# The start of a convolution-and-MLP kernel: first fifteen blocks in groups of five, x ahead of the third w_in chunk, more dummy matmuls, band cast on ScalarE

## The chip, the cores and the metric

One core of one Trainium2 chip. The metric is the device time of one execution in microseconds (us), lower is better. The kernel before took 723.87 us (median of three runs, 723.49 to 724.0).

## The reference, cut to what matters

```python
# a causal convolution of width 7 over the sequence, one softmaxed filter per head, 8 heads of 24 channels
w = softmax(weight)                                   # [8, 7]
y[b, s, h, :] = sum_k w[h, k] * x_pad[b, s + k, h, :] # x: [8, 4096, 192]
# an MLP without biases on its result
h = y.reshape(32768, 192) @ w_in                      # [192, 2048]
g = h * cos(h)
out = g @ w_out                                       # [2048, 192]
```

## The kernel before: the parts that the change touches

Two sequences of the batch are worked on side by side, one in each half of the 128 partitions ("lanes"). The convolution is a matmul with a banded matrix (`band`) over blocks of 112 positions; 37 blocks make a sequence. Eight 64-channel slices of blocks ("a pair") fill one PSUM bank per lane. A group of eight blocks gives three pairs; a group of five gives two, one of 28 matmuls (channel slices 0 and 1 of four blocks) and one of 40 (the fifth block and slice 2):

```python
def group(b, k, n):
    if n == 5:
        pairs.append([(b, k + j, c) for c in range(2) for j in range(4)])
        pairs.append([(b, k + 4, c) for c in range(NCH)] + [(b, k + j, 2) for j in range(4)])
    elif n == 2:
        ...
    else:
        pairs.extend([(b, k + j, c) for j in range(n)] for c in range(NCH))
    loads.extend((b, k + j, min(4, n - j)) for j in range(0, n, 4))   # x comes in loads of up to 4 blocks

for b in range(HB):
    k = 0
    for n in [8] * (NBLK // 8) + [5] if b else [5, 8, 2] + [8] * ((NBLK - 21) // 8) + [6]:
        group(b, k, n)
        k += n
```

The order of the loads on SyncE's queue (every buffer is one of eight staging buffers; w_in comes in four chunks, w_out in two):

```python
load_blocks(*loads[0], (nc.sync, nc.scalar)); load_blocks(*loads[1])
load_w1(0); load_w1(1)
load_w1(2)
load_ahead(1)          # the x of the next pair: both loads of the eight-group
...
load_w1(3); load_w2(0); load_w2(1)
```

The rest is a hand-made schedule. Each letter emits one step: `U` an up-projection (6 matmuls, one of 512 positions by 128 hidden columns on both lanes), `S` its cosine on ScalarE, `M` the product on VectorE, `C`/`c` the two halves of a pair's convolution, `e` its copy out of PSUM and its transposing DMA into `cT`, `p` the cast of another pair's x and the loads for the next, `d` one of the sixteen parts of a down-projection (8 matmuls), `x`/`y` the stores, `k` the next of the jobs of `later()`, which are all on GpSimd or SyncE:

```python
def later():
    yield from (lambda c=c, q=q: cast_w1(c, q) for c in range(1, 3) for q in range(NCH))
    yield cast_pair
    yield lambda: load_ahead(3)
    yield cast_pair
    yield cast_pair
    yield from (lambda q=q: cast_w1(3, q) for q in range(NCH))
    yield from (lambda c=c, q=q: cast_w2(c, q) for c in range(2) for q in range(4))

fill("kkkUSMUSMUSMkkkUSMUSMUSMkkUSMUSMCceUSMkkkkkCceUSMUSMkkkkkkkkCceUSMU")
for k in range(NSETS - 2):
    emit("dddSMdUdMSUdSdMUdSMd" + ("p" if k == 0 else "") + "UdMSUdSdMCcdedMUdpSdUyxUMS")
```

I call the part up to the first `d` the fill and each pass of the loop a turn (8 `U`, 16 `d`). The down-projection changes between two PSUM banks, and at each changeover TensorE waits for a "mark", a 1x1 memset on GpSimd; GpSimd does its casts and marks in program order. And SyncE issues x loads, transposes and stores from one queue, also in program order.

## Time and profile before

| what | value | where from |
|---|---|---|
| time | 723.87 us | median of 3 runs |
| TensorE busy | 708.5 of 722.6 us | busy table |
| TensorE first useful up-projection | 12.67 us | timeline |
| first down-projection | 32.50 us | timeline |
| turns 2, 3, 4 start | 43.46, 54.37, 65.27 us | timeline |

From the first down-projection on, a turn takes 10.9 us and TensorE has no gap in it. (The times of a trace are of one execution; that of the kernel before took 724.41 us.)

### The profile page before, as it was taken

Reading aid. Unit: us, or ns where it says so; the run is one execution under the profiler, and the core shown is the slowest. Engines: PE = TensorE matmul, PEld = TensorE weight load, DVE = VectorE, ACT = ScalarE, POOL = GpSimd, SP = SyncE. Lnnn points to the kernel's source line nnn. Section 1 sums busy time; section 2 is a strip of 40 time slices with the busy share of each in tenths; the row PEclk is TensorE's granted clock in tenths of the full one; section 3 lists DMA queues with packets and bytes.
Section 4 is the critical chain, followed back from the end, with each engine's and each line's share of the span. In section 5 each row is a group of like instructions: output and inputs, shape, how many; then the busy total and the mean of one; then the engine's idle time right before and its main releaser. Section 6 shows DMA issues by size and latency. Waiting matters only on the chain.

```text
span 722.6 us, 27515 instructions
## 1 busy us (share of the span) xinstructions
PE 708.5 (98%) x12284; PEld 527.0 (73%) x12284; DVE 641.3 (89%) x594; ACT 589.1 (82%) x641; POOL 95.0 (13%) x345
## 2 busy tenths in 40 slices
PE   7799999999999999999999999999999999999997
PEld 5477777777777777777777777777777777777776
DVE  5799899999989999898898998998998999999994
ACT  4788888888888888888888888888888888778773
POOL 4510111110110111111101111101101100000000
PEclk9999999999999999999999999999999999999999
DMA  9956333552827337254653554516273321011102
GB/s 233 239 124 149 83 90 101 113 128 67 159 37 158 53 106 158 63 129 99 116 129 83 93 111 108 137 58 159 49 146 82 85 64 56 27 43 45 46 25 67
DMA packets 126339, 72.58 MB, mean 100 GB/s; under 512 B 52428, under 2 KB 124684, under 8 KB 126220
## 3 DMA queue, kind: packets, MB, share of 16 engines
q1 hardware_dynamic: 125386, 70.23, 42.4%
q8 instruction: 96, 1.57, 0.9%
q10 hardware_dynamic: 834, 0.59, 0.3%
q14 instruction: 23, 0.19, 0.1%
HBM read 33.48 MB, written 25.17 MB: 81 GB/s over the span
## 4 chain that ended last, share of the span: by engine, by line
PE 96%; DMA 3%; SPq 1%; DVE 0%; ACT 0%; issue 0%; POOL 0%; POOLq 0%
PE h L286 49%; PE acc L286 46%; DMA xw<-in_x_dram 2%; DMA xw<-in_moe_w_in_dram 1%; SPq L110 0%; DVE g L396 0%; SPq L232 0%; ACT cos L391 0%; POOL xb L161 0%; SPq L230 0%; DVE osb L433 0%; ACT osb L433 0%; SPq L104 0%; POOLq L542 0%; POOL mark L296 0%
## 5 line engine op out<-in xcount | busy, mean ns | idle before, releaser
L396 DVE TENSOR_TENSOR g<-h,cos 128x1024 bf16<-128x1024 f32 x512 | 603.8, 1220 | 30.1 <-ACT cos L391 23.4
L391 ACT ACTIVATE cos<-h 128x1024 bf16<-128x1024 f32 x512 | 511.1, 1023 | 106.7 <-PE h L286 87.5
L286 PEld LDWEIGHTS <-g 64*128 64x128 bf16 x8192 | 353.1, 94 | 102.3 <-POOL mark L296 2.2
L286 PE MATMUL acc<-w,g 64*128 64x192 bf16 x8064 | 415.3, 243 | 0.3 <-POOL mark L296 0.3
L286 PE MATMUL h<-cT,w 64*128 64x512 bf16 x3072 | 409.3, 378 | 2.2 <-DVE g L396 2.1
L286 PEld LDWEIGHTS <-w 64*128 64x128 bf16 x3072 | 148.4, 94 | 79.6 <-issue 5.8
L296 POOL MEMSET mark<- 1x1 f32 x192 | 16.9, 88 | 602.6 <-PE acc L286 593.8
L433 DVE COPY osb<-acc 128x384 f32<-128x384 f32 x63 | 35.1, 558 | 39.6 <-PE acc L286 39.6
L161 POOL CAST xb<-xw 128x512 bf16<-128x512 f32 (+1 forms) x113 | 64.7, 603 | 13.1 <-DMA xw<-in_x_dram 11.9
L344 ACT CAST ct<-h 112x1024 bf16<-112x1024 f32 (+2 forms) x53 | 52.5, 990 | 8.8 <-PE h L286 5.0
L286 PEld LDWEIGHTS <-band 64*128 64x128 bf16 x952 | 31.3, 96 | 5.0 <-issue 4.1
L433 ACT COPY osb<-acc 128x384 f32<-128x384 f32 x63 | 29.8, 473 | 5.7 <-PE acc L286 5.7
L286 PE MATMUL h<-xb,band 64*128 64x192 bf16 (+10 forms) x912 | 34.2, 214 | 0.0
L235 POOL CAST w<-xw 128x512 bf16<-128x512 f32 x12 | 6.9, 613 | 5.3 <-DMA xw<-in_moe_w_in_dram 5.3
L286 PE MATMUL h<-w,g 64*128 64x192 bf16 x128 | 5.9, 243 | 0.3 <-POOL mark L296 0.3
L183 PE MATMUL acc<-unit 128*112 128x112 bf16 x46 | 4.8, 302 | 1.3 <-POOL unit L166 1.3
L286 PE MATMUL acc<-xb,band 64*128 64x192 bf16 (+2 forms) x40 | 2.5, 260 | 3.5 <-POOL xb L161 3.4
L342 ACT CAST ct<-acc 112x512 bf16<-112x512 f32 x6 | 3.2, 592 | 3.0 <-PE acc L286 3.0
L183 PEld LDWEIGHTS <-unit 128*112 128x112 bf16 x46 | 4.4, 211 | 1.4 <-POOL unit L166 1.3
L245 POOL CAST w<-xw 128x384 bf16<-128x384 f32 x8 | 3.7, 507 | 0.3 <-DMA xw<-in_moe_w_out_dram 0.3
L196 ACT ACT_TABLE_LOAD x1 | 1.3, 1283 | 2.6 <-issue 2.6
L344 DVE CAST ct<-h 112x896 bf16<-112x896 f32 x1 | 1.1, 1091 | 2.1 <-PE h L286 2.1
(37 smaller groups left out, 18.7 us busy)
## 6 DMA issues: line engine op xcount, KB each, us to landing
out_dram<-osb SPq DMA_DIRECT2D x63, 384.0 KB, 2.9
xw<-in_x_dram SPq DMA_DIRECT2D x62, 384.0 KB, 6.3
xw<-in_x_dram SPq DMA_DIRECT2D x7, 336.0 KB, 4.2
xw<-in_moe_w_in_dram SPq DMA_DIRECT2D x4, 512.0 KB, 7.7
xw<-in_moe_w_out_dram SPq DMA_DIRECT2D x2, 768.0 KB, 8.9
cT<-ct SPq DMA_TRANSPOSE x66, 2.7
xw<-in_moe_w_in_dram SPq DMA_DIRECT2D x8, 128.0 KB, 8.4
xw<-in_x_dram SPq DMA_DIRECT2D x2, 192.0 KB
```

The lines of the kernel that those rows point to most:

```text
L161: copies[j % len(copies)](out=xbs[p][:, s0:s1], in_=src)
L183: nc.tensor.matmul(out=acc[0][0:W, 0:W], lhsT=unit, rhs=unit, start=True, stop=True)
L196: nc.scalar.activation(out=wex, in_=wq, func=AF.Exp)
L235: copy(out=w1[:, q, c * CW:(c + 1) * CW], in_=staged[1, c][:, q, :])
L245: nc.gpsimd.tensor_copy(out=w2[:, c * n:(c + 1) * n, :][:, fs, :], in_=staged[2, c][:, fs, :])
L286: ins = nc.tensor.matmul(out=o, lhsT=w, rhs=r, start=start, stop=stop, skip_group_check=True)
L296: ins = nc.gpsimd.memset(mark, 0.0)
L342: copy(out=ct[0:W, 0:n, s, :], in_=bank[0:W, 0:n * L].rearrange("p (j c) -> p j c", c=L))
L344: copy(out=ct[0:W, 0:n].rearrange("p j s c -> p s j c"), in_=ps[0:W, :, 0:n * L].rearrange("p s (j c) -> p s j c", c=L))
L391: nc.scalar.activation(out=cos, in_=hs[n], func=AF.Sin, bias=math.pi / 2.0, scale=1.0)
L396: nc.vector.tensor_tensor(out=g, in0=hs.pop(n), in1=cs.pop(n), op=ALU.mult)
L433: copy(out=osbs[k][:, 2 * bank:2 * bank + 2, :].rearrange("p a d -> p (a d)"), in_=src[:, 0:2 * D])
```

## The change

Its intent: convolve less before the up-projections can go on (the first pair of a group of five needs four blocks' x, 786 KB, that of a group of eight needs eight), have that x on the way before the third chunk of w_in, keep the clock that TensorE is granted up with more dummy matmuls, whose results nobody reads, and free VectorE of one copy.

```diff
-        for n in ... [5, 8, 2] + [8] * ((NBLK - 21) // 8) + [6]:
+        for n in ... [5, 5, 5] + [8] * ((NBLK - 21) // 8) + [6]:
...
-    keep_warm(30)
+    keep_warm(56)
...
-    nc.vector.tensor_copy(out=band[:, :, V:W], in_=spread)
-    keep_warm(16)
+    nc.scalar.copy(out=band[:, :, V:W], in_=spread)
+    keep_warm(20)
...
+    load_ahead(1)
     load_w1(2)
-    load_ahead(1)
+    load_ahead(2)
...
     def later():
-        yield from (lambda c=c, q=q: cast_w1(c, q) for c in range(1, 3) for q in range(NCH))
+        yield from (lambda q=q: cast_w1(1, q) for q in range(NCH))
         yield cast_pair
-        yield lambda: load_ahead(3)
+        yield from (lambda q=q: cast_w1(2, q) for q in range(NCH))
         yield cast_pair
-        yield cast_pair
+        yield lambda: load_ahead(2)
...
-    fill("kkkUSMUSMUSMkkkUSMUSMUSMkkUSMUSMCceUSMkkkkkCceUSMUSMkkkkkkkkCceUSMU")
-    for k in range(NSETS - 2):
-        emit("dddSMdUdMSUdSdMUdSMd" + ("p" if k == 0 else "") + "UdMSUdSdMCcdedMUdpSdUyxUMS")
+    fill("kkkUSMUSMUSMkUSMUSMkkkUSCceMUSMUSMkUSMkUSCceMUSMkkkkkkkkkkkUSMU")
+    emit("dddSMdUdMpSUdSdMUdSMdUdMSCcpUedSdMCcdedMUdpSdUyxUMS")
+    for k in range(1, NSETS - 2):
+        emit("dddSMdUdMSUdSdMUdSMdUdMSUdSdMCcdedMUdpSdUyxUMS")
```

More of the change, by code (lines that the diff above doesn't have):

```diff
@@ L129 @@
         k = 0
-        for n in [8] * (NBLK // 8) + [5] if b else [5, 8, 2] + [8] * ((NBLK - 21) // 8) + [6]:
+        for n in [8] * (NBLK // 8) + [5] if b else [5, 5, 5] + [8] * ((NBLK - 21) // 8) + [6]:
             group(b, k, n)
```

## The prediction

> **What bounds the kernel now.** I read the page first: the busy table and the chain that ended last.
>
> ```profile
> PE 708.5 (98%) x12284; PEld 527.0 (73%) x12284; DVE 641.3 (89%) x594; ACT 589.1 (82%) x641; POOL 95.0 (13%) x345
> PE 96%; DMA 3%; SPq 1%; DVE 0%; ACT 0%; issue 0%; POOL 0%; POOLq 0%
> ```
>
> TensorE is busy 98% of the span and is 96% of the chain, so the steady state is a TensorE program. The diff touches only the start. A start-up change can return just the time in which TensorE does no useful work there, so the second view was a table of windows over the first 45 us (columns: window, length, busy us and count of PE, PEld, DVE, ACT, POOL, then granted clock, DMA share, GB/s).
>
> ```profile
> 12.70:24.50 11.80, 7.77 (x48) 3.06 (x48) 9.70 (x9) 8.05 (x8) 4.07 (x7) 1.00 1.09 247
> 24.50:25.44 0.94, 0.00 (x1) 0.00 (x1) 0.02 (x1) 0.00 (x0) 0.67 (x2) 1.00 1.09 341
> 26.10:29.50 3.40, 3.38 (x30) 1.73 (x28) 1.23 (x1) 3.14 (x5) 3.40 (x7) 0.50 1.10 346
> 34.47:45.00 10.53, 10.53 (x215) 8.25 (x212) 9.73 (x10) 9.07 (x10) 2.17 (x7) 1.00 0.77 166
> ```
>
> From 34.47 us on TensorE never stops. Before that there are three losses: 12.70 to 24.50 it is one third idle, at 24.50 to 25.44 every compute engine but GpSimd stands still, and from 26.10 to 29.50 it runs at half clock. What holds it is told by the chain of waits in order of time (start, length, what):
>
> ```profile
> 13.31 11.34 DMA xw<-in_x_dram
> ...
> 24.77 0.62 POOL xb L161
> 25.39 0.04 issue
> 25.44 0.62 PE acc L286 x12
> ...
> 29.52 1.03 ACT cos L391
> 30.56 0.02 issue
> 30.58 1.24 DVE g L396
> 31.82 0.04 issue
> 31.86 0.82 PE h L286 x6
> ```
>
> So the third group of pairs (an eight-block group, whose x fills two staging buffers and stands behind the third w_in chunk) lands near 24.65. Its convolution sits in TensorE's program after eight up-projections, so everything behind it waits. The third view is the timeline of the start:
>
> ```profile
> 1.33 3.05 PE L183 MATMUL acc<-unit 128*112 128x112 bf16 x30 [1.33 <-POOL unit L166]
> 6.42 0.53 PE L215 MATMUL acc<-near,slide 14*128 14x64 bf16 x7 [2.04 <-DVE near L211]
> 6.88 1.74 PE L183 MATMUL acc<-unit 128*112 128x112 bf16 x16
> 8.55 1.94 PE L286 MATMUL h<-xb,band 64*128 64x96 bf16 x68
> 12.67 3.68 PE L286 MATMUL h<-cT,w 64*128 64x512 bf16 x18 [0.15 <-ACT cT L490]
> 16.51 0.82 PE L286 MATMUL h<-cT,w 64*128 64x512 bf16 x6 [0.16 <-DVE g L396]
> 25.44 0.62 PE L286 MATMUL acc<-xb,band 64*128 64x192 bf16 x12 [3.43 <-POOL xb L161]
> ```
>
> A dummy costs 3.05/30 = 0.10 us. Three up-projections take 3.68 us, though one in a row costs 0.65 us later in the chain: TensorE is at half rate until about 15.9 us, although the clock column, which starts from the first recorded change, still says 1.00.
>
> **What the Trainium skill says.** "TensorE: Matmul & The Clock Gate", Part 1, "What's actually happening": TensorE starts at half clock, is released after about 3.4 us of sustained work, is throttled again after an idle window of that length, and the window runs free. The trace agrees: 30 dummies (3.05 us) and a 2.04 us hole do not release it, the gap of 3.43 us throttles it and the slow stretch is 3.4 us long. The same page's table of engine queues has GpSimd strictly first-in, first-out; here that matters because its casts of weights and x and the 1x1 "mark" that TensorE waits for between output halves share one line. "DMA: Bandwidth & Descriptors", "Issuing engines are not separate DMA queues": all issues share the same 16 DMA engines. The trace agrees (DMA share 1.09 from 12.70 to 24.50), so moving x ahead must push the third w_in chunk back.
>
> **The change, part by part.**
>
> (1) Dummies, 30 to 56 and 16 to 20. At 0.10 us, 56 run from 1.33 to 7.0 us and close the hole. I expect release somewhere in 4.8 to 8.2 us, not 15.9, depending on the window's phase. If it comes near 5.6, the last 14 run at about half cost, the spread matmuls still start near 6.45 and 20 quick dummies end near 8.0. If it comes last, the dummies end near 8.9 and delay the convolution by 0.4 us. Warm, the 68 first matmuls should cost 1.13 us, not 1.94 (a 28-matmul pair costs 0.50 and a 40-matmul pair 0.63 at 279 and 290 us), the 15 transposes perhaps 0.5 us less.
>
> (2) Band cast to ScalarE. Removes 0.62 us from VectorE at 6.99 and puts about 0.55 on an idle ScalarE (a 128x448 copy out of PSUM took 0.53 there). VectorE starts its x casts near 7.1 instead of 7.53. But GpSimd's two casts, 7.08 to 8.44, still end last for the second pair. Worth 0.4 us for the first pair only.
>
> (1) and (2) together: first convolution 8.0, ct copies (1.01 and 1.09 us) done by 10.3, transposes 10.9, cT copied 11.6. First up-projection 11.4 instead of 12.67 and warm: its cosine starts near 12.1 instead of 14.17, the first product at 13.1 instead of 15.23. That is 2.1 us earlier for VectorE, which paces this stretch at 1.16 us a product.
>
> (3) Group of five and order of transfers. Before the next convolution can start, only four blocks (786 KB) must land, right behind w_in chunk 1, instead of eight behind chunk 2. Bytes: x alone went at about 215 GB/s and w_in at about 340. Chunk 1 is in at about 12.3, 786 KB of x takes 3.65 us more, and landings trailed the bulk of the bytes by 3 to 4 us in this stretch (nearly all of chunk 2's packets are through by 14.0, its last at 17.1; GpSimd gets the first x at 21.56): landing near 19.0, two casts of 0.61, convolution near 20.3 instead of 25.44. By then products 0 to 5 are done (13.1 + 6 x 1.16 = 20.1). Then 1.1 us of warm convolution, 1.07 of ct copies and a cosine before the next product, near 23.2. VectorE therefore still idles about 3 us, but TensorE's hole is about 2.5 us and no full window is idle: no second half-clock stretch (saves 3.4 x 0.5 = 1.7 us of TensorE work, mostly under VectorE's pace). Chunk 2 lands near 21 instead of 17 and is cast by 22.8, about when up-projection 8 wants it.
>
> (4) w_out. Ahead of it stand 590 KB less x, 2.6 us: w_out's first half lands near 26.2 (28.6 now), the second near 29, cast until about 31. Thirteen up-projections are out near 28.5 (VectorE: 23.2 + 4 x 1.18 = 27.9 for product 9, which frees the last buffer). The down-projection, 32.50 now, then starts at about 28.7. Its fifth part (34.47 now) waits for the first mark, behind GpSimd's w_out casts: about 31.3 to 31.6. Gain there 2.9 to 3.2 us.
>
> (5) What is paid. Taken from the start of one group of matmuls to the start of what follows it, in the warm loop, an eight-block group costs TensorE 0.44 + 0.45 + 0.44 = 1.33 us, the two-block pair 0.50 (at 39.70), a five-group 0.50 + 0.63 = 1.13. Before, the fill holds an eight-group and the first loop turn the two-block pair; after, the fill holds one five-group and the first turn another. What the fill gains or loses is in (3) and (4) already; behind the start of the steady state TensorE has 1.13 - 0.50 = 0.63 us more to do.
>
> Sum: -3.05 (the middle of (4)) + 0.63 = -2.4 us; 723.87 - 2.4 = 721.4.
>
> **Rivals.** *Nothing comes out of it.* A later w_in chunk 2, or transposes that reach SyncE's queue behind the new x loads (a four-block transpose takes 1.2 us to issue, an eight-block one 2.3), could replace the wait at 25.44. I work out the second group's transposes landing at 32.5 to 33.5 and the up-projection that reads them at 34. Against: 0.5 us margin. If lost: 723 to 724. *VectorE becomes the bound.* 641.3 us of work, and 9.73 busy in 10.53; it ends no waits of TensorE after 34.47, and in the new plan it is ahead by about one product. Unlikely; would cap the gain at some 2 us. *The landings don't trail.* If x lands at 16.5, VectorE never stops, and only w_out limits: gain 4 to 4.5 us, 719.5.
>
> **Range and chances.** Landing time of the first x transfer (19.0, +-1.5 us) moves nearly one for one into the end until w_out's landing takes over; clock phase adds +-0.5. I take 719.8 to 723.3. A 2% step is 14.5 us, more than the whole start up to the steady state could give: within 2% at 0.98. A new stall large enough for 2% would need a bad buffer cycle; 0.01.
>
> **What would show it.** Clock: first record of full clock before 8.2 us and no half-clock stretch at 26. The first up-projection near 11.4, three of them in about 2.1 us. First product 13.1. The second group's convolution near 20. Down-projection start near 28.7, fifth part before 31.7 with a wait on the mark. Later turns of 10.9 us unchanged. I am wrong if the steady state starts less than 1 or more than 5 us earlier, or if TensorE waits again after 35 us.

## The result, and the profile after

The changed kernel took 723.67 us (median of four runs, 723.4 to 724.35), the kernel before 723.68 in its four. The ratio of the two is 1.0005, 95% interval 0.9987 to 1.0022. A ratio here is the mean time of one kernel's fast runs over that of the other's of the same rounds, so it is not quite the ratio of the medians. Nothing was gained; I had put the time at 721.4 and in the range 719.8 to 723.3.

The page of the changed kernel, busy table and chain:

```profile
PE 707.8 (98%) x12370; PEld 527.0 (73%) x12370; DVE 640.9 (89%) x593; ACT 589.4 (82%) x641; POOL 95.0 (13%) x344
PE 95%; DMA 2%; DVE 1%; ACT 1%; issue 0%; ACTq 0%; POOL 0%; POOLq 0%
```

The totals are those of before, 86 matmuls more (30 dummies and 56 of the convolution). They cannot tell where anything went. The timeline of TensorE in the changed kernel can:

```profile
1.33 4.60 PE L183 MATMUL acc<-unit 128*112 128x112 bf16 x56 [1.33 <-POOL unit L166]
...
11.85 2.12 PE L287 MATMUL h<-cT,w 64*128 64x512 bf16 x18 [0.33 <-ACT cT L491]
...
18.09 0.41 PE L287 MATMUL acc<-xb,band 64*128 64x96 bf16 x12
...
26.45 1.50 PE L287 MATMUL acc<-w,g 64*128 64x192 bf16 x32
...
29.57 0.50 PE L287 MATMUL acc<-w,g 64*128 64x192 bf16 x8 [0.98 <-POOL mark L297]
...
34.72 0.82 PE L287 MATMUL h<-cT,w 64*128 64x512 bf16 x6 [2.02 <-DMA cT<-ct]
```

Up to the first down-projection everything the change was made for has come, and more than I predicted: three up-projections take 2.12 us instead of 3.68 (the clock records full clock from 4.74 us on, not from 15.87), the second group is convolved from 18.09 instead of 25.44, the first down-projection starts at 26.45 instead of 32.50. That is a lead of 6.05 us. Then two waits that the kernel before did not have: 0.98 us for a mark and 2.02 us for `cT`, the transposed convolution of the second group ("the hole" below). The table of windows, one line per turn (columns as in the prediction), changed kernel first:

```profile
26.45:43.00 16.55, 13.55 (x246) 10.06 (x244) 10.37 (x10) 10.23 (x12) 5.76 (x14) 0.90 1.25 186
43.00:53.91 10.91, 10.91 (x191) 8.32 (x189) 9.92 (x10) 9.29 (x11) 1.94 (x6) 1.00 0.43 81
```

and the kernel before:

```profile
32.50:43.46 10.96, 10.96 (x218) 8.47 (x216) 9.75 (x10) 9.32 (x11) 2.74 (x9) 1.00 0.90 193
43.46:54.37 10.91, 10.91 (x191) 8.41 (x189) 9.92 (x10) 9.29 (x11) 2.00 (x6) 1.00 0.27 72
```

The first turn takes 16.55 us instead of 10.96; the second is alike. So 5.59 of the 6.05 us are lost in one turn and the remaining 0.46 us stay to the end (turns 3, 4 and 57 start 0.46 us earlier too). That is less than the run-to-run spread of either kernel.

Why `cT` is late is in the list of what SyncE issues in the changed kernel (start, length of the issue with its wait, what):

```profile
18.96 1.01 SPq L240 DMA_DIRECT2D xw<-in_moe_w_out_dram  x2
20.20 5.52 SPq L372 DMA_TRANSPOSE cT<-ct  x2
25.81 2.65 SPq L110 DMA_DIRECT2D xw<-in_x_dram  x4
28.56 2.52 SPq L372 DMA_TRANSPOSE cT<-ct  x2
```

The first two transposes hold the queue from 20.20 to 25.72, behind them stand four x loads for the third group, and behind those the transposes of the pair that the 17th up-projection needs. They are issued by 31.08 and land at 34.58; TensorE was there at 32.7. The hole has a second cost. The clock records show 3.41 us at half clock from 35.46 on. The Trainium skill's page "TensorE: Matmul & The Clock Gate", Part 1, "What's actually happening", says that the clock falls after an idle window of about 3.4 us. Here it fell after a window (32.05 to 35.46) that was not idle:

```profile
32.05:35.46 3.41, 1.39 (x25) 0.86 (x23) 2.23 (x2) 1.02 (x1) 1.17 (x2) 1.00 1.25 157
```

TensorE was busy for 1.39 of its 3.41 us. (I take the clock's windows to be 3.41 us long, back to back: the full clock before lasted from 4.74 to 35.46, which is nine times 3.41.)

From the fifth part of the first down-projection, 29.57 us, to turn 2 the changed kernel takes 13.43 us and the kernel before 8.99. The lines, with the same stretch of a second execution of the changed kernel that had no half clock (after_again, below) in the middle:

```profile
29.57:43.00 13.43, 11.40 (x206) 8.51 (x208) 7.25 (x8) 7.84 (x10) 3.03 (x7) 0.87 1.28 187
29.71:41.96 12.25, 9.98 (x206) 7.15 (x208) 7.22 (x7) 7.55 (x9) 3.02 (x7) 1.00 1.17 200
34.47:43.46 8.99, 8.99 (x180) 6.82 (x178) 8.23 (x9) 7.56 (x9) 1.56 (x6) 1.00 0.86 185
```

The difference of 4.44 us is 2.03 us of idle time, the hole alone, and 2.41 us more of busy time. Without half clock the busy time is 0.99 us above the kernel before, so 1.42 us go to the half clock.

My theory at this point: the change brings the first down-projection forward, but not what the first turn itself needs. All of the first 15 blocks' x, all weights and the second group's transposes are needed by the end of the first turn in both kernels. The change leaves the x of five of these blocks to that turn, where the kernel before left two, together with their convolutions and casts. The rivals: the DMA engines are simply full, so no order helps; the half clock is the loss; VectorE or ScalarE limits the first turns.

### The profile page after: what moved, and what is told of

The parts are those of the page before. It is cut to its first block, busy times and chain, and to the rows that moved or that the text cites. A ratio compares the mean times of both kernels' runs of the same rounds, so it can differ in the third digit from the quotient of the medians.

```text
span 721.9 us, 27691 instructions
## 1 busy us (share of the span) xinstructions
PE 707.8 (98%) x12370; PEld 527.0 (73%) x12370; DVE 640.9 (89%) x593; ACT 589.4 (82%) x641; POOL 95.0 (13%) x344
## 4 chain that ended last, share of the span: by engine, by line
PE 95%; DMA 2%; DVE 1%; ACT 1%; issue 0%; ACTq 0%; POOL 0%; POOLq 0%
PE h L287 49%; PE acc L287 46%; DVE g L397 1%; DMA cT<-ct 1%; DMA xw<-in_x_dram 1%; ACT cos L392 0%; ACT ct L345 0%; POOL xb L161 0%; ACTq L80 0%; PE acc L487 0%; DVE osb L434 0%; ACT cT L490 0%; ACT osb L434 0%; ACT cT L491 0%; ACTq L104 0%
## 5 line engine op out<-in xcount | busy, mean ns | idle before, releaser
L287 PE MATMUL h<-xb,band 64*128 64x192 bf16 (+11 forms) x940 | 34.9, 212 | 0.4 <-DVE xb L161 0.3
L287 PEld LDWEIGHTS <-band 64*128 64x128 bf16 x1008 | 31.6, 95 | 1.4 <-issue 1.0
```

What stands on the lines that cost most here:

```text
L287: ins = nc.tensor.matmul(out=o, lhsT=w, rhs=r, start=start, stop=stop, skip_group_check=True)
```

## The experiments

Twelve kernels in three calls, five rounds each, each call with its own runs of the kernel before (median 723.73, 723.55 and 724.13 us). All gave the right result. The numbers of each trace that I compare:

| run | median us | ratio to before (95%) | first `d` | turn 2 starts | turn 1 | turn 4 starts |
|---|---|---|---|---|---|---|
| kernel before | 723.87 | | 32.50 | 43.46 | 10.96 | 65.27 |
| changed kernel | 723.67 | 1.0005 (0.9987 to 1.0022) | 26.45 | 43.00 | 16.55 | 64.81 |
| after_again | 723.48 | 0.9991 (0.9978 to 1.0005) | 26.49 | 41.96 | 15.47 | 63.77 |
| t_first | 724.26 | 1.0007 (0.9995 to 1.0020) | 26.50 | 43.32 | 16.82 | 65.13 |
| clock_fill | 724.88 | 1.0012 (0.9999 to 1.0025) | 27.20 | 42.99 | 15.79 | 66.42 |
| t_first_conv_later | 723.24 | 0.9996 (0.9980 to 1.0012) | 27.44 | 41.03 | 13.59 | 63.76 |
| dummies_only | 724.49 | 1.0009 (0.9995 to 1.0022) | 32.14 | 43.10 | 10.96 | 65.34 |
| few_dummies | 724.27 | 1.0003 (0.9990 to 1.0015) | 27.05 | 44.06 | 17.01 | 65.87 |
| no_conv_first_turn | 720.92 | 0.9960 (0.9947 to 0.9972) | 26.61 | 37.90 | 11.29 | 61.78 |
| no_conv_mark_early | 720.25 | 0.9950 (0.9938 to 0.9963) | 26.68 | 37.51 | 10.83 | 61.35 |
| conv_later_only | 724.04 | 1.0002 (0.9989 to 1.0016) | 26.27 | 41.55 | 15.28 | 65.39 |
| x_behind_chunk2 | 724.51 | 1.0008 (0.9996 to 1.0020) | 31.69 | 43.71 | 12.02 | 65.52 |
| band_on_vector | 723.79 | 0.9996 (0.9984 to 1.0008) | 26.53 | 43.09 | 16.56 | 64.90 |
| best_few_dummies | 720.95 | 0.9953 (0.9941 to 0.9965) | 27.05 | 37.51 | 10.46 | 61.35 |

Turn 4 is the fair place to compare: where convolutions are moved between turns, they are all done by then.

**after_again**: the changed kernel unaltered.

> The changed kernel as it is, once more, so that the others of this call have it on the same chip. Both theories: ratio to the kernel before 0.998 to 1.002. If the half-clock stretch near 35 us depends on the phase of the clock's window, some executions will show a mean clock of 0.999 instead of 0.997, and by theory 'the half clock costs its full 1.7 us' those would be about 1.5 us shorter; the one such execution so far was only 0.3 us shorter, which speaks against it.

Its profiled execution has the same waits (`cT` at 34.86) but no half clock: a boundary of the clock's windows, near 33.6 (full clock came at 6.31 us, and eight times 3.41 us later is 33.6), fell into the hole, and the window before it held 2.64 us of matmuls. The first turn took 15.47 instead of 16.55 us, 1.08 us less: 1.42 us less of busy time (12.13 after 13.55), and 0.34 us more of short waits, so by the busy time the half clock cost 1.42 us and not 1.7. The six runs agree roughly: the three with a mean clock of 0.999 took 722.62, 722.17 and 723.33, the three with 0.997 or 0.998 took 723.64, 723.62 and 723.79, on average 1.0 us more. In the four runs of the first call the one with 0.999 took 723.4, the others 0.5 us more on average. Whether it happens depends on the execution. What remains without it is still a first turn of 15.47 us.

**t_first**: the second group's transposes ahead of the third group's x loads.

```diff
         yield cast_pair
-        yield lambda: load_ahead(2)
         yield from (lambda q=q: cast_w1(3, q) for q in range(NCH))
+        yield lambda: load_ahead(2)
```

> Only the order on SyncE's queue is changed: the transposes of the second five-group are issued before the four x loads of the third. Theory A (order of issue: the 17th up-projection waits because the transposes stand behind those loads): transposes issued from 25.8 instead of 28.6, landed by 32 instead of 34.6, the wait of 2.0 us for cT is gone and no half-clock stretch follows; but the x of the third group comes some 2.5 us later, so its convolution in the first loop turn (35.9 now) may wait for the cast: gain 1 to 3 us, time 721 to 722.7. Rival B (the transposes land late because the DMA engines are full with w_out and x): landing still at 34 or later, wait still there, time as the changed kernel, 723.5.

The transposes landed at 29.51 and the 17th up-projection ran at 33.02 without a wait: that the engines are simply full is wrong for them. But the time did not fall. TensorE and GpSimd of this run:

```profile
33.67 0.49 PE L287 MATMUL acc<-w,g 64*128 64x192 bf16 x8
35.81 0.41 PE L287 MATMUL h<-xb,band 64*128 64x96 bf16 x12 [1.65 <-POOL xb L161]
```

```profile
35.15 1.17 POOL L161 CAST xb<-xw 128x512 bf16<-128x512 f32 x2 [5.14 <-DMA xw<-in_x_dram]
36.25 0.09 POOL L297 MEMSET mark<- 1x1 f32 x1
```

The x loads, now issued 3 us later, were cast from 35.15 on, and the convolution that stands in the first turn waited for them in the place of the up-projection. One wait took the place of the other, with the half clock behind it as before. My expectation saw this wait but took it for the smaller of the two. All six runs (723.89 to 725.28) lie above the six of after_again (722.17 to 723.79).

**clock_fill**: 30 dummies in the hole, so that the clock stays up.

```diff
     def up(n):
...
+        if n == NF:
+            for _ in range(30):
+                nc.tensor.matmul(out=h[0:W, 0, 0:W], lhsT=unit, rhs=unit, start=True, stop=True)
```

> 30 dummy matmuls (about 1.7 us at full clock) into the PSUM tile that the 17th up-projection then overwrites, in the hole in which it waits for cT. The wait itself stays. Theory: part of the loss is the half clock from 35.5 to 38.9 that the hole brings. If it costs what it seems, 3.4 x 0.5 = 1.7 us, the time falls by 1.2 to 1.7 us; if something else paces the first loop turn (casts of x, marks), by under 0.4 us, with the full clock in the records all the same.

The dummies ran from 33.83 to 35.58, the clock records show full clock throughout, and the time did not fall. Its first turn took 15.79 us, near the 15.47 of after_again, which had no half clock either. The profiled execution lost time elsewhere: w_out was there for GpSimd only at 26.64 (25.44 in the changed kernel), and turn 2 took 12.52 us with a wait of 1.44 us that the profile gives no cause for. That can't be luck alone: all six runs (723.86 to 725.53) lie above all six of after_again (722.17 to 723.79), by 1.4 us in the medians. Why the dummies cost time stays open. The half clock is a loss of 1.0 to 1.4 us in some executions; it is not where 5.6 us went.

**t_first_conv_later**: t_first, and the extra convolution goes into the second turn.

```diff
-    emit("dddSMdUdMpSUdSdMUdSMdUdMSCcpUedSdMCcdedMUdpSdUyxUMS")
-    for k in range(1, NSETS - 2):
+    emit("dddSMdUdMSUdSdMUdSMdpUdMSUdSdMCcdedMUdpSdUyxUMS")
+    emit("dddSMdUdMSUdSdMUdSMdUdMSCcpUedSdMCcdedMUdpSdUyxUMS")
+    for k in range(2, NSETS - 2):
```

> As t_first, and the extra convolution of the third five-group moves from the first loop turn to the second, where its x has long been cast. Theory A: no wait of TensorE for cT nor for casts in the first turn, first turn 11.0 to 12.5 us instead of 16.55, start of the second turn near 38.5 to 39.5 instead of 43.0, less 0.6 us for the convolution moved into the second turn: time 719.8 to 721.0. Rival B: still waits for cT, time 722.5 or more.

The first turn fell to 13.59 us, not to between 11.0 and 12.5. One convolution and its cast were still in the first turn, and GpSimd, in order, stood at that cast with the mark behind it (GpSimd, then TensorE of this run):

```profile
35.35 1.17 POOL L161 CAST xb<-xw 128x512 bf16<-128x512 f32 x2 [5.19 <-DMA xw<-in_x_dram]
36.45 0.09 POOL L297 MEMSET mark<- 1x1 f32 x1
```

```profile
36.60 0.83 PE L287 MATMUL acc<-w,g 64*128 64x192 bf16 x16 [1.64 <-POOL mark L297]
```

So the late x reaches TensorE in two ways, through its own convolution and through a down-projection that has nothing to do with it. The time, 723.24 us over a wide 722.51 to 725.72, is not separable from the kernel before.

**no_conv_first_turn**: t_first, and nothing in the first turn needs the third group's x.

```diff
-    emit("dddSMdUdMpSUdSdMUdSMdUdMSCcpUedSdMCcdedMUdpSdUyxUMS")
-    for k in range(1, NSETS - 2):
+    emit("dddSMdUdMSUdSdMUdSMdUdMSUdSdMdedMUdpSdUyxUMS")
+    for k in range(2):
+        emit("dddSMdUdMSUdSdMUdSMdUdMSCcpUedSdMCcdedMUdpSdUyxUMS")
+    for k in range(3, NSETS - 2):
```

> As t_first (transposes ahead of the x loads), and the first loop turn has no convolution and one cast only at its end, so that nothing in it needs the third group's x; two convolutions in each of turns 2 and 3. Theory (the lead of 6 us at the first down-projection is lost only because the first turn needs 590 KB of x that was put off, in TensorE's order and in GpSimd's queue ahead of the mark): no wait for cT or x, only the first mark's 1 us; first turn 11.4 to 12 us instead of 15.5 to 16.5; second turn starts near 38.2, fourth near 61 (65.3 before, 64.8 changed): time 719.0 to 720.2. Rival (DMA share or VectorE limits the first turns whatever the order): second turn not before 40, time above 721.5.

The first turn took 11.29 us, turn 2 started at 37.90, and the time fell to 720.92 us, ratio 0.9960 with an interval that ends at 0.9972. This is the lead, let out. It is 0.7 us above my range because turns 2 and 3, with two convolutions each, took 12.04 and 11.84 us where my reckoning (10.44 us of projections, 16 x 0.33 + 8 x 0.645, and 1.13 or 0.89 of convolutions) gave 11.57 and 11.33; one wait of 0.30 us in turn 2 and one of 0.29 in turn 3 are the larger part of it. The rival that DMA share or VectorE limits the first turn whatever the order has fallen.

**no_conv_mark_early**: the same, and the last four w_out casts stand behind the first mark.

```diff
-    fill("kkk ... kUSCceMUSMkkkkkkkkkkkUSMU")
-    emit("dddSMdUdMSU ...
+    fill("kkk ... kUSCceMUSMkkkkkkkUSMU")
+    fill("dddSMdkkkkUdMSU ...
```

> As no_conv_first_turn, and GpSimd's last four w_out casts are issued behind the first mark instead of before it. Theory: the wait of 1 us on the mark goes, but the ninth part of the down-projection may wait for the second half of w_out instead: 0.3 to 1.0 us less than no_conv_first_turn, time 718.3 to 719.8. Rival: no difference, because the casts then block something else.

720.25 us (719.88 to 720.5), 0.67 us below no_conv_first_turn by the medians, and no run of the one overlaps the other. The step is as I wrote, the time is above my 718.3 to 719.8, since no_conv_first_turn was above its range. The wait on the mark is gone from TensorE's timeline. Its first two turns, to be held against the two tables above:

```profile
26.68:37.51 10.83, 10.83 (x177) 8.00 (x178) 9.75 (x10) 7.86 (x10) 3.98 (x12) 1.00 0.77 155
37.51:49.53 12.02, 11.87 (x247) 9.07 (x244) 10.00 (x10) 10.10 (x12) 3.07 (x9) 1.00 0.76 169
```

This version beats the kernel before by 0.5%, and by the ratios the changed one too. It was run at another time.

**conv_later_only**: the turns of no_conv_first_turn, but x loads still ahead of the transposes.

```diff
-    emit("dddSMdUdMpSUdSdMUdSMdUdMSCcpUedSdMCcdedMUdpSdUyxUMS")
-    for k in range(1, NSETS - 2):
+    emit("dddSMdUdMSUdSdMUdSMdUdMSUdSdMdedMUdpSdUyxUMS")
+    for k in range(2):
+        emit("dddSMdUdMSUdSdMUdSMdUdMSCcpUedSdMCcdedMUdpSdUyxUMS")
+    for k in range(3, NSETS - 2):
```

> The changed kernel with the convolutions of the third five-group moved out of the first loop turn (two each in turns 2 and 3), but the x loads still ahead of the second group's transposes on SyncE's queue. With t_first (transposes first, convolution in turn 1: second turn at 43.3) and no_conv_first_turn (both: 37.9) this makes the square. Theory (two waits in series, either of which alone keeps the lead from coming out): wait of about 2 us for cT stays, no wait for x, first turn 13 to 14.5 us, second turn at 39.5 to 41, time 721.5 to 723. Rival (only the convolution matters, the transposes are free once it is gone): second turn before 38.5, time under 721.2.

The wait for `cT` stayed. The view of who waited for whom, 26 to 55 us of this run (total, times, longest):

```profile
PE h L287 <- DMA cT<-ct: 2.0, 1, 2.0
```

No wait for x is left, and yet turn 1 took 15.28 us and the time was 724.04: worse than my 13 to 14.5 us and 721.5 to 723. The half clock (35.39 to 38.80 in this run) again followed the hole and, by after_again, would account for 1.0 to 1.4 us of it. With t_first and no_conv_first_turn it closes the square. By the start of turn 4: changed kernel 64.81 (63.77 without half clock), transposes first alone 65.13, convolutions later alone 65.39, both 61.78. Neither alone gains anything, both together 3 us, or 2 us against the execution without half clock. That is what two waits, one in front of the other, look like: one for the transposes, one for the x loads of the same queue.

**dummies_only**: the kernel before with 56 and 20 dummies.

```diff
-    keep_warm(30)
+    keep_warm(56)
...
-    keep_warm(16)
+    keep_warm(20)
```

> The kernel before with only the 56 and 20 dummy matmuls. Theory (the opening up to 25 us is paced by the landing of the third group's x, so a warm TensorE alone has nothing to win): full clock recorded before 9 us instead of 15.9, first up-projection some 0.7 us earlier, but the third group's convolution still near 25.4 and the first down-projection within 0.5 us of 32.5; time within 0.4 us of the kernel before. Rival (the clock was a loss of its own): first down-projection 1.5 us or more earlier and the time lower by as much.

Full clock from 4.90 us, first up-projection at 11.23 instead of 12.67, and the third group's convolution at 24.87, the first down-projection at 32.14: of 1.4 us only 0.4 are left. By turn 4 they are gone as well. The time, 724.49, is not separable from before. The x landing set the fill; a faster TensorE only waits longer for it (and is at half clock from 21.96 to 28.79, after a window with 1.13 us of matmuls in 3.41).

**few_dummies**: the changed kernel with 30 and 16.

```diff
-    keep_warm(56)
+    keep_warm(30)
...
-    keep_warm(20)
+    keep_warm(16)
```

> The changed kernel with the old 30 and 16 dummies. Theory (first loop turn is paced by x and transposes, which the clock does not touch): the start is slower by 1 to 2 us (first down-projection 27 to 29 instead of 26.5), but the wait for cT near 33 shrinks by nearly as much; start of the second turn within 0.7 us of 42 to 43, time within 0.5 us of the changed kernel. Rival: the dummies' 2 us come out at the end, time 1.5 us or more above the changed kernel.

The first down-projection was 0.6 us later, at 27.05, not 1 to 2 us. In this execution the 30 dummies did bring full clock, at 5.03 us; it was half again from 8.44 to 15.27. That the wait for `cT` would shrink was wrong: the transposes landed later too (35.69 after 34.58). The first turn took 17.01 us with the half clock, and turn 2 started at 44.06, later than I wrote. The time, 724.27, against 723.48 of after_again; the ratios' intervals overlap. It was run at another time. What the dummies are worth in this kernel stays below what these runs resolve.

**x_behind_chunk2**: the second group's x behind the third w_in chunk again.

```diff
-    load_ahead(1)
     load_w1(2)
+    load_ahead(1)
     load_ahead(2)
```

> The changed kernel with the x of the second five-group behind the third w_in chunk again, as before the change. Theory (the early x buys a lead at the first down-projection that the first turn does not let out): second group's convolution at 21 to 22.5 instead of 18.1, first down-projection 2 to 3.5 us later than 26.5, but the second turn starts within 1.2 us of 42 to 43.3 and the time is within 0.8 us of the changed kernel. Rival: the time rises by 2 us or more.

This is the clearest undoing. The second group's convolution came at 22.42 and the first down-projection at 31.69, 5.2 us later than in the changed kernel (I had said 2 to 3.5: VectorE ran dry for 5.2 us waiting for a cosine, and the clock fell to half from 21.68 to 28.51). Turn 2 then started at 43.71, 0.7 us later than in the changed kernel, and 1.8 us later than in after_again, which like this run had no half clock in the first turn. 5.2 us at the first down-projection are worth 0.7 to 1.8 us one turn later.

**band_on_vector**: the band cast back on VectorE.

```diff
-    nc.scalar.copy(out=band[:, :, V:W], in_=spread)
+    nc.vector.tensor_copy(out=band[:, :, V:W], in_=spread)
```

> The changed kernel with the band cast back on VectorE. In the changed profile x arrived at 7.8 us on both engines that cast it, after the band cast had ended at 7.35, so its move should be worth nothing: first convolution within 0.3 us of 8.0 to 8.3, and the sine table load can come earlier on ScalarE; first down-projection within 0.3 us of 26.5, time within 0.4 us of the changed kernel.

First down-projection 26.53, turn 2 at 43.09, 723.79 us: nothing. In the changed kernel both x casts started at 7.8, when x had landed, and the band copy had ended at 7.35 on ScalarE.

**best_few_dummies**: no_conv_mark_early with 30 and 16 dummies.

```diff
-    keep_warm(56)
+    keep_warm(30)
...
-    keep_warm(20)
+    keep_warm(16)
```

> no_conv_mark_early (720.25 us, first down-projection 26.7) with the old 30 and 16 dummies, to see what the dummies are worth where the first turn no longer hides it. few_dummies started its down-projections 0.6 us later than the changed kernel. Theory: 0.3 to 1.0 us more, time 720.5 to 721.3. Rival: nothing, as w_out's landing near 26 sets the first down-projection anyway: 719.9 to 720.4.

Its down-projections start at 27.05 instead of 26.68, but turn 2 starts at 37.51 in both, which is what the rival says. By the medians it is 0.7 us slower, which would fit my theory; the two ratios, 0.9953 and 0.9950, differ by 0.2 us, and each interval is 0.9 us wide to either side. It was run at another time. So what more dummies bring to the better version is not settled.

## Why the prediction was wrong, point by point

- **What bounds the kernel before.** Right: TensorE in the steady state, and the landing of the third group's x in the fill. dummies_only shows it.
- **Part (1) and (2), dummies and band.** The clock came at 4.74 us, a little before my 4.8 to 8.2. First convolution 8.27 (8.0 predicted), first up-projection 11.85 (11.4), first product 13.76 (13.1). The Trainium skill's page "TensorE: Matmul & The Clock Gate", Part 1, "What's actually happening", was of use here: the trace agrees with its 3.4 us of sustained work, with the release 3.41 us after the first dummy. In the ten other runs with 56 dummies it came 2.92 to 5.96 us after it (4.25 us in band_on_vector, 7.29 in no_conv_first_turn), so the delay isn't fixed, which fits the free-running window of the page. And that 30 dummies do not release the clock, as I read in the trace before, was a matter of the execution: in few_dummies and best_few_dummies they did, at 5.03 and 5.06 us. The band cast is worth nothing, as band_on_vector shows, where I had 0.4 us for the first pair; x landed later than I took it (cast at 7.8, not 7.1).
- **Part (3), five blocks and the order of transfers.** Mechanism right, size too small. I had the first x landing near 19.0 because landings trailed by 3 to 4 us before; it was cast from 17.42, and the convolution came at 18.09, not 20.3.
- **Part (4), first down-projection at about 28.7, fifth part at 31.3 to 31.6.** 26.45 and 29.57. The wait on the mark was predicted and is there, 0.98 us. The gain at the fifth part was 4.9 us (34.47 to 29.57), not 2.9 to 3.2.
- **Part (5) and the sum, "-3.05 + 0.63": the step that failed.** I took the gain at the fifth part of the first down-projection as final and charged what follows with 0.63 us of matmuls only. It was charged with 4.44: the lead was 4.90 us there and 0.46 at the start of turn 2. The terms, by the three lines above, are 2.03 for the wait for `cT`, 1.42 for the half clock that followed it, and 0.99 for more work, where I had 0.63 (the other 0.36 us of busy time I have not taken apart). The wait and the half clock had no term in my sum; the wait stood among the rivals, as unlikely.
- **The first rival.** I named the very wait, transposes behind the new x loads, worked out a landing at 32.5 to 33.5 and a need at 34, and called it 0.5 us of margin. The landing was 34.58, behind the x loads: in t_first, ahead of them, it was 29.51. That the first two transposes held SyncE's queue for 5.52 us, where two of 1.2 us each would have been 2.4, adds to it; no run takes it away. And the need was 32.7, *earlier* because the fill went better than predicted. A lead moves every deadline behind it forward; I moved only the start.
- **What I did not see at all.** That the same x has a second and a third way to the end, its convolution in the first turn and the mark behind its cast. The fill needs 590 KB less, but the first turn needs as much in total as before: blocks 0 to 14 are convolved by its end in both kernels. The work was put off, not taken away. no_conv_first_turn takes it out of the turn, to where it is not needed sooner (its positions are first read in the third turn), and 2 to 3 us come out. That the time fell into the 723 to 724 of the first rival is in part luck: it named one of the two waits, and taking away that one alone (t_first) gains nothing.

Not settled: why the first transpose of the fill took 4.2 us to issue where others of its size took 1.2 (the profile names ScalarE's cosine, while its own input was copied by 20.17), and why turns with two convolutions take 0.5 us more than their matmuls. For the first there is a hint: in all eleven runs with this order of loads that issue ended 0.95 to 1.05 us before the first half of w_out landed (24.43 and 25.38 in the changed kernel, 25.62 and 26.59 in clock_fill), whenever it began. The transfers ahead of it are thus a likelier reason than a cosine, but no run tests it.

## What to carry to other kernels

A gain at the start reaches the end only if everything that the next stage reads is ready earlier too: after working out the new start of a stage, list what that stage reads (transposes, weights, marks, casts) with its landing, and hold each against the deadline as moved. Where undoing a part costs 5 us at one point and only 1 or 2 at the next, look for a wait between the two; where taking away one wait gains nothing, look for a second behind it before giving up the theory. On in-order queues, put a transfer that is merely early behind one that is soon needed.

## What the Trainium skill lacked or had wrong

- "TensorE: Matmul & The Clock Gate", Part 1, "What's actually happening": gives one idle window of about 3.4 us as what throttles the clock. Here it was throttled after windows with 1.39 us (changed kernel) and 0.66 us (kernel before, 22.69 to 26.10) of matmuls in 3.41 us, and was not after one with 2.47 us. The busy time alone doesn't decide it: the clock fell after 2.03 us (few_dummies, 5.03 to 8.44) and not after 1.78 (t_first_conv_later, 33.85 to 37.27). The other way, a window 92% busy with short matmuls and with waits between them did not release it, while one with 2.92 us of dummies, 86%, did (band_on_vector, 0.84 to 4.25). The line of the kernel before, 9.04 to 12.45 us (two windows before its release at 15.87):

```profile
9.04:12.45 3.41, 3.15 (x77) 2.50 (x72) 1.62 (x2) 1.80 (x3) 1.73 (x3) 1.00 1.06 305
```

  The page has no share of a window that counts as busy or idle; where it names short idles as a cause, under "A second HAM failure mode: psum-queue depth-cycling", it gives no figure either.
- The same page puts the penalty under "Terms" at the throttled time times one minus the clock share; by that rule I estimate 1.7 us for 3.41 us at half clock. Between two executions of the changed kernel, one with it and one without, TensorE's busy time in the first turn differed by 1.42 us and the turn by 1.08. One pair of executions doesn't show the rule wrong; how much of the penalty reaches the time, the page doesn't say.
- "DMA: Bandwidth & Descriptors", "Bandwidth": its table is for 128 partitions and goes by size alone. In the changed kernel x, 768 bytes a row into 64 partitions a transfer, moved at 211 GB/s (12 to 14 us), and w_out, also 768 bytes a row but into 128 partitions, at 369 GB/s (23 to 26 us), both with the engines' busy share at 1.1. The page's "Rules for kernel authors" advise one transfer over 128 partitions instead of two over halves, without a rate for the halves. The cause was not tested.
- No page that I read gives in us how long a transposing DMA of such a size holds its queue: 1.2 us for four blocks, 2.3 for eight, and 3.3 to 5.3 for the first one of the fill in the eleven runs with the new order of loads.
